# Transposing the probabilities of the last 64 queries of two heads together, and the first two query tiles in one bank, in a block-causal attention kernel with a gated feed-forward

## The chip, the cores and the metric

The kernel runs on one core of one Trainium2 chip. The metric is device time in microseconds of one execution, the median of several runs; lower is better. The engines that work side by side are TensorE (PE in the profile; its weight loads are PEld), VectorE (DVE), ScalarE (ACT), GpSimd (POOL), and SyncE (SP), which here issues transfers. TensorE's results go to PSUM, a memory of eight banks, from which DVE and ACT read them ("evict" them) into SBUF, the working memory.

## What is computed

Attention over 8 batches, 8 heads, 576 tokens and 64 features, in which a query of 64-token block i sees the keys of blocks 0 to i; then a feed-forward network on the concatenated heads, with a convolution of three taps along the tokens as a gate:

```python
scores = scale * np.matmul(q, k.transpose(0, 1, 3, 2))
mask = block_i >= block_j                       # blocks of 64 tokens
scores = np.where(mask, scores, -1000000000.0)
attn = np.exp(scores - np.max(scores, axis=-1, keepdims=True))
attn = attn / (np.sum(attn, axis=-1, keepdims=True) + 1e-09)
x = np.matmul(attn, v)                          # heads side by side: 512 features
...
h = np.maximum(x @ w_in, 0.0)                   # 512 -> 1024
conv_out += conv_w[k][None, None, :] * hp[:, k:k + S, :]   # k = 0, 1, 2
gate = 1.0 / (1.0 + np.exp(-conv_out))
return (h * gate @ w_out).astype(np.float32)    # 1024 -> 512
```

All is float32. To keep precision at TensorE's faster float32r rate, the kernel splits a float32 operand into a high part (rounded to float32r) and a low part (the rest), and sums the products high x high, high x low and low x high.

## The kernel before

**Tiling.** Heads are worked in 32 pairs (two heads of a batch), 64 heads in all. The 576 queries of a head are cut into four tiles of 128 and a last one of 64. Query tile i (0 to 3) sees 128 (i + 1) keys; the last 64 queries see all 576. The last 64 queries of both heads of a pair share one tile of 128 partitions, block 4: rows 0 to 63 belong to the first head and rows 64 to 127 to the second. Their scores and their softmax are made once for the pair, in the first head's turn.

**Stages.** `stage_t` loads q and k of a pair, transposes them (line 476), and splits them (lines 480 and 483) into tiles that transfers copy to where they are needed. `stage_s` makes a head's scores (lines 581, 583; for block 4 line 619), masks (586), takes row maxima (589, 622), exponentials with row sums (592, 633), the reciprocal of the sums (555, 560) and the normalised probabilities `p0` to `p4` (566, on POOL). `stage_x` transposes the probabilities on PE (line 660), so that keys lie along the partitions, and evicts each tile twice: ACT copies the high part out of PSUM (682) and DVE subtracts it from what stands in PSUM to give the low part (685). Tiles 0 and 1 go to `ptah` and `ptal`, tiles 2, 3 and block 4 to `ptbh` and `ptbl`, as [partition, four chunks of 128 keys, 320 queries]. The fifth chunk of keys (64 keys, block 4 alone) stands in an unused corner, chunk 3, columns 0 to 63: its high part on partitions 0 to 63, its low part on 64 to 127. `stage_pv` multiplies by v (725, 732) and evicts into `xt` (743, 746). For the first eight heads, tiles 2 and 3 have their low part made by PE and ACT instead (689, 693), and some banks come from another group.

`ffn` runs for half a batch at a time once the batch's eight heads are done: the first matmul (line 780) for eight groups of 128 features, each with its activation and gate (795 to 821, on ACT, DVE and POOL), and the second matmul (840) with its eviction (850). It runs beside the next batch's attention.

**What sets the order.** No loop is run as written: every step is recorded with an engine, an estimated duration (`c_mm`, `c_act`, `c_dve`, `c_pool`), what it depends on, and a due time. `Plan.order` then simulates the engines with these durations and writes the instructions out, on each engine in the order in which the simulation started them. The feed-forward matmuls are "paced": they fill PE between the others. So an estimated duration that changes can move any instruction. Each engine works its queue in order.

**Buffers.** PSUM's eight banks are given out in three groups: two to `s` (scores), three to `f` (feed-forward), three to `w`, which the transposes of q and k, of the probabilities (`pt`) and the products with v (`tv`) share in turn. `ptah`, `ptal`, `ptbh` and `ptbl` have one buffer each, for all heads in turn.

Of the kernel before, what the change touches and what calls it, by code (L numbers as in the profile page):

```python
# [10 lines left out]
F32R = mybir.dt.float32r  # L11
# [136 lines left out]
def kernel(  # L148
# [85 lines left out]
    def c_dve(n, fast=False):  # L234
        return 0.065 + n / (1920.0 if fast else 960.0)
# [206 lines left out]
    def stage_t(nat, at, first=False):  # L442
# [22 lines left out]
        for which, (n, ld) in enumerate(nat):  # L465
# [4 lines left out]
            for j in range(2):  # L470
# [16 lines left out]
                o = pl.op(ACT, c_act(HS), ev_hi, t0 + 0.5 * j + 0.3, deps=[o], bufs=[tb, hi])  # L487
                es.append(o)
                es.append(pl.op(DVE, c_dve(HS), ev_lo, t0 + 0.5 * j + 0.7, deps=[o], bufs=[tb, hi, lo]))
# [51 lines left out]
    def stage_s(ops, hh, at, early, shared):  # L541
# [8 lines left out]
        def finish(blocks, st, c0, t0):  # L550
# [11 lines left out]
            o = pl.op(DVE, 0.08, i1, t0, deps=exps[4] if blocks[0] == 4 else [exps[x] for x in blocks], bufs=[st])  # L562
            o = pl.op(DVE, 0.09, i2, t0, deps=[o], bufs=[st])
# [8 lines left out]
        for i in range(4):  # L572
# [25 lines left out]
            exps.append(pl.op(ACT, c_act(nk, True, True, True), ex, t0 + 0.6, deps=[o], bufs=[sb, st, pt]))  # L598
# [32 lines left out]
        for j in range(2):  # L631
            def ex4(j=j, sb=banks[j]):
                nc.scalar.activation(out=p4.ap[:, HS * j:HS * j + HS], in_=sb.ap[:, 0:HS], func=AF.Exp,  # L633
                                     bias=st4.ap[:, 2:3], accum_out=st4.ap[:, 4 + j:5 + j])

            es.append(pl.op(ACT, c_act(HS, True, True, True), ex4, t0 + 0.6, deps=[o], bufs=[banks[j], st4, p4]))
# [9 lines left out]
    def stage_x(pbd, hh, at, early):  # L646
        pb, done = pbd
        ta = [one([P, 384], F32R, nm) for nm in ("ptah", "ptal")]
        tb_ = [one([P, 4, 320], F32R, nm) for nm in ("ptbh", "ptbl")]
        evs = []  # L650
        for i in range(5):
            t0 = at + 1.1 * i
            tb = bank("f" if early and i in EFPT else "pt")
            nq = 128 if i < 4 else 64

            def tr(i=i, tb=tb, nq=nq):
                r = slice(64 * hh, 64 * hh + 64) if i == 4 else slice(0, P)
                for c in range(i + 1):
                    kk = 128 if c < 4 else 64
                    nc.tensor.matmul(tb.ap[0:kk, c * nq:(c + 1) * nq], pb[i].ap[r, 128 * c:128 * c + kk],  # L660
                                     ident[r, r], start=(c == 0), stop=True, is_transpose=True,
                                     skip_group_check=True)

            o = pl.op(PE, (i + 1) * (0.109 if i < 4 else 0.056), tr, t0, deps=[done[i]], bufs=[tb, pb[i]])
            nc4 = min(i + 1, 4)

            pth, ptl = ta if i < 2 else tb_

            def chunks(x, i=i, nq=nq, nc4=nc4):
                if i < 2:  # L670
                    return x.ap[:, 128 * i:256 * i + 128].rearrange("p (c n) -> p c n", c=nc4)
                return x.ap[:, 0:nc4, 128 * i - 256:128 * i - 256 + nq]

            parts = [(P, 0, nc4, lambda chunks=chunks, x=pth: chunks(x), lambda chunks=chunks, x=ptl: chunks(x), ptl)]
            if i == 4:
                parts.append((64, 4 * nq, 1, lambda x=pth: x.ap[0:64, 3:4, 0:64], lambda x=pth: x.ap[64:P, 3:4, 0:64], pth))
            for kk, col, nn, hi, lo, lo_t in parts:
                def src(tb=tb, kk=kk, col=col, nn=nn, nq=nq):
                    return tb.ap[0:kk, col:col + nn * nq].rearrange("p (c n) -> p c n", c=nn)

                def ev_hi(src=src, hi=hi):
                    nc.scalar.activation(out=hi(), in_=src(), func=AF.Copy)  # L682

                def ev_lo(src=src, hi=hi, lo=lo):
                    nc.vector.tensor_tensor(out=lo(), in0=src(), in1=hi(), op=ALU.subtract)  # L685

# [271 lines left out]
```

## Time and profile before

| | |
|---|---|
| median of 3 runs | 878.92 us (873.92 to 879.34) |
| profiled execution: its time, its span, mean granted TensorE clock | 879.45 us, 877.7 us, 0.972 |
| half transposes of block 4 (line 660), 64 rows by 128 and 64 keys | 256 + 64 in the trace |
| transposes of 128 x 128 into `w` banks (line 660) | 608 in the trace |
| evictions on ACT (line 682) and on DVE (line 685) in the program | 384 and 368 |

A row of the view by shapes reads: line, engine, operation, output <- input, shapes, count | busy microseconds, mean nanoseconds of one | idle time of the engine before them and what ended it. A row of the view by windows reads: the stretch, its length, then for each engine its busy microseconds and number of instructions, the granted clock, and the transfers' share and GB/s. The chain of waits follows the last instruction back to what released it; a row gives the start, the length and the work. Some matmul records can be missing from a trace, so counts there may fall short of the program's.

### The profile page before, as it was taken

What the parts mean: (1) busy time and instruction counts of PE and PEld (TensorE: products, weight loads), DVE (VectorE), ACT (ScalarE), POOL (GpSimd) and SP (SyncE); (2) the same over time, 40 slices, a digit from 0 to 9 for tenths busy, and PEclk for the clock granted to TensorE, in tenths of its full rate; (3) what the DMA queues carried; (4) which work ended last, traced back from release to release, by engine and by line L of the source; (5) the groups of instructions that cost most, each with busy time, mean ns of one, the idle gap of its engine ahead of it and who ended that gap; (6) DMA issues with size and microseconds to landing.
All of it is one profiled execution on the core that took longest, in us unless ns stands there. A gap on an engine that the chain in (4) does not pass through costs nothing.

```text
span 877.7 us, 17654 instructions
## 1 busy us (share of the span) xinstructions
PE 833.4 (95%) x5393; PEld 726.3 (83%) x5393; DVE 682.9 (78%) x2044; ACT 633.6 (72%) x1894; POOL 463.2 (53%) x615
## 2 busy tenths in 40 slices
PE   4988887899999999999999999999999999999998
PEld 3766776788888979888898979888888979898996
DVE  6677899989796967879796867878796867878541
ACT  5676666678696867878696867878696857878552
POOL 2466786766455434656465434556455534556331
PEclk9987787999999999999999999999999999999999
DMA  8565461554444355454445255454445255540001
GB/s 202 148 159 136 111 182 49 136 134 99 116 102 104 78 135 124 111 131 102 112 94 127 66 136 124 111 133 105 108 101 127 61 136 124 122 99 2 25 24 37
DMA packets 162865, 95.11 MB, mean 108 GB/s; under 512 B 132156, under 2 KB 136276, under 8 KB 162772
## 3 DMA queue, kind: packets, MB, share of 16 engines
q1 hardware_dynamic: 161588, 93.69, 43.9%
q8 instruction: 44, 0.72, 0.4%
q10 hardware_dynamic: 1184, 0.30, 0.2%
q14 instruction: 49, 0.40, 0.1%
HBM read 37.77 MB, written 9.44 MB: 54 GB/s over the span
## 4 chain that ended last, share of the span: by engine, by line
PE 65%; DVE 20%; ACT 10%; issue 3%; DMA 1%; POOL 1%; ACTq 0%; SPq 0%; DVEq 0%; POOLq 0%
PE f L840 19%; PE f L780 11%; PE w L725 8%; PE w L660 8%; PE s L581 4%; PE s L583 3%; PE w L840 3%; DVE st L589 3%; DVE t L802 2%; PE w L476 2%; DVE t L806 2%; DVE ptbl L685 2%; PE s L619 2%; ACT p L592 2%; ACT p L633 2%
## 5 line engine op out<-in xcount | busy, mean ns | idle before, releaser
L566 POOL TENSOR_SCALAR p<-p,st 128x128 f32<-128x128 f32 (+4 forms) x288 | 163.0, 579 | 198.2 <-DVE st L560 125.5
L592 ACT ACTIVATE p<-s,st 128x128 f32<-128x128 f32 (+3 forms) x256 | 134.9, 527 | 55.0 <-DVE st L589 52.3
L821 POOL TENSOR_TENSOR gl<-t,gh 128x288 fp32r<-128x288 f32 x128 | 103.4, 810 | 129.8 <-ACT gh L818 117.7
L660 PE MATMUL w<-ident,p 128*128 128x128 f32 (+1 forms) x928 | 141.3, 266 | 8.2 <-DVE ql L483 2.9
L660 PEld LDWEIGHTS w<-ident,p 128*128 128x128 f32 (+1 forms) x928 | 98.3, 141 | 41.2 <-issue 14.4
L589 DVE TENSOR_REDUCE st<-s 128x1 f32<-128x128 f32 (+3 forms) x256 | 123.5, 484 | 4.4
L682 ACT ACTIVATE ptbh<-w 128x384 fp32r<-128x384 f32 (+3 forms) x248 | 97.0, 419 | 18.2 <-PE w L660 16.9
L840 PE MATMUL f<-woh,gh 128*128 128x512 f32 x248 | 104.4, 421 | 0.0
L685 DVE TENSOR_TENSOR ptbl<-w,ptbh 128x512 fp32r<-128x512 f32 (+1 forms) x176 | 95.2, 541 | 7.7 <-ACT ptbh L682 6.5
L780 PE MATMUL f<-xh,wih 128*128 128x290 f32 x480 | 100.3, 314 | 0.8 <-POOL xh L254 0.3
L780 PE MATMUL f<-xh,wil 128*128 128x290 f32 x480 | 100.1, 313 | 0.0
L840 PE MATMUL f<-wol,gh 128*128 128x512 f32 x248 | 98.6, 398 | 0.0
L840 PE MATMUL f<-woh,gl 128*128 128x512 f32 x248 | 98.6, 398 | 0.0
L780 PE MATMUL f<-xl,wih 128*128 128x290 f32 x480 | 97.3, 309 | 0.0
L583 PE MATMUL s<-kl,qz 128*128 128x128 f32 (+3 forms) x256 | 86.5, 338 | 0.0
L743 ACT ACTIVATE xt<-w 64x256 f32<-64x256 f32 (+1 forms) x128 | 51.3, 401 | 42.8 <-PE w L725 37.6
L780 PEld LDWEIGHTS f<-xh,wih 128*128 128x128 f32 x480 | 74.8, 192 | 5.4 <-DVE t L814 2.2
L802 DVE SCALAR_TENSOR_TENSOR t<-f,cw,t 128x287 f32<-128x287 f32 (+1 forms) x120 | 61.1, 509 | 18.8 <-ACT t L798 17.7
L780 PEld LDWEIGHTS f<-xh,wil 128*128 128x128 f32 x480 | 74.3, 193 | 1.5
L780 PEld LDWEIGHTS f<-xl,wih 128*128 128x128 f32 x480 | 73.8, 192 | 1.1
L746 DVE TENSOR_TENSOR xt<-w,xt 64x256 f32<-64x256 f32 x112 | 51.6, 461 | 26.4 <-ACT xt L743 23.4
L811 ACT ACTIVATE t<-t 128x288 f32<-128x288 f32 x128 | 56.4, 440 | 13.7 <-DVE t L806 13.5
(158 smaller groups left out, 2033.4 us busy)
## 6 DMA issues: line engine op xcount, KB each, us to landing
qn<-in_q_dram SPq DMA_DIRECT2D x64, 144.0 KB, 3.1
out_dram<-stage SPq DMA_DIRECT2D x36, 256.0 KB, 2.3
kn<-in_k_dram SPq DMA_DIRECT2D x62, 144.0 KB, 3.0
ka<-kh SPq DMA_DIRECT2D x62, 144.0 KB, 2.7
kb<-kh SPq DMA_DIRECT2D x62, 144.0 KB, 2.6
vn<-in_v_dram SPq DMA_DIRECT2D x64, 128.0 KB, 2.7
qa<-qh SPq DMA_DIRECT2D x31, 144.0 KB, 3.1
qa<-ql SPq DMA_DIRECT2D x31, 144.0 KB, 3.0
```

The costliest lines, as they stand in the source:

```text
L566: nc.gpsimd.tensor_scalar(out=pt.ap, in0=pt.ap, scalar1=st.ap[:, col:col + 1], scalar2=0.0, op0=ALU.mult, op1=ALU.add)
L583: nc.tensor.matmul(sb.ap[:, 0:nk], qz.ap[:, z:z + 128], kl.ap[:, 0:nk], start=False, stop=True)
L589: nc.vector.tensor_reduce(out=st.ap[:, i:i + 1], in_=sb.ap[:, 0:nk], op=ALU.max, axis=AX.X, negate=True)
L592: nc.scalar.activation(out=pt.ap[:, 0:nk], in_=sb.ap[:, 0:nk], func=AF.Exp, bias=st.ap[:, i:i + 1], accum_out=st.ap[:, 4 + 2 * i:5 + 2 * i])
L660: nc.tensor.matmul(tb.ap[0:kk, c * nq:(c + 1) * nq], pb[i].ap[r, 128 * c:128 * c + kk], ident[r, r], start=(c == 0), stop=True, is_transpo ...
L682: nc.scalar.activation(out=hi(), in_=src(), func=AF.Copy)
L685: nc.vector.tensor_tensor(out=lo(), in0=src(), in1=hi(), op=ALU.subtract)
L725: nc.tensor.matmul(tb.ap[0:m, q0 - qa:qb - qa], vv.ap[:, c, hh, w[part]], pm.ap[:, 128 * c + q0:128 * c + qb] if qa == 0 else pm.ap[:, c, ...
L780: nc.tensor.matmul(fb.ap[:, 0:n2], wt[:, c, fs], xs[c][xi].ap[:, x0:x0 + n2], start=(n + c - c0 == 0), stop=(n + c - c0 == 3 * NCC - 1))
L802: nc.vector.scalar_tensor_tensor(out=t.ap[:, i0:], in0=fb.ap[:, own + i0 - 1:own + HS - 1], scalar=cw[:, f:f + 1], in1=t.ap[:, i0:], op0=A ...
L821: nc.gpsimd.tensor_tensor(out=gbuf[1].ap[:, f, carry:carry + HS], in0=t.ap, in1=gbuf[0].ap[:, f, carry:carry + HS], op=ALU.subtract)
L840: nc.tensor.matmul(fb.ap[:, 0:DM], gbuf[a].ap[:, f, cs], w[:, f, :], start=(f == 0 and n == 0), stop=(f == NFC - 1 and n == 2))
```

## The change

Three things change.

1. *Block 4 once per pair.* In the first head's turn `stage_x` now transposes block 4 with all its 128 rows: four transposes of 128 rows by 128 keys and one of 128 rows by 64 keys, where each head had four of 64 rows by 128 keys and one of 64 by 64. One eviction pair moves 512 columns out of PSUM into both heads' tiles, another the 128 columns of the fifth chunk. The second head's turn transposes tiles 0 to 3 only.
2. *Tiles 0 and 1 together.* The one transpose of tile 0 and the two of tile 1 go into one bank and leave it with one eviction pair of 384 columns instead of 128 and 256.
3. *Buffers and costs.* `ptbh` and `ptbl` become one tile each with a half for each head, so that two heads no longer take turns on one buffer. And the planner's estimates rise: 0.05 us for DVE work with two tensor inputs, 0.02 to 0.08 for several ACT steps, and more for the sums and reciprocals.

Per pair there are 25 transposes where there were 30, and eight eviction pairs where there were twelve; the number of elements moved is the same. The lines move: 660 becomes 672, 725 and 732 become 749 and 756, 743 and 746 become 767 and 770, 780 becomes 804, 795 to 821 become 819 to 845, 840 becomes 864, 850 becomes 874; 682 and 685 stay.

```diff
-    def c_dve(n, fast=False):
-        return 0.065 + n / (1920.0 if fast else 960.0)
+    def c_dve(n, fast=False, two_in=False):
+        return 0.065 + n / (1920.0 if fast else 960.0) + (0.05 if two_in else 0.0)
...
-            o = pl.op(DVE, 0.08, i1, t0, deps=exps[4] if blocks[0] == 4 else [exps[x] for x in blocks], bufs=[st])
-            o = pl.op(DVE, 0.09, i2, t0, deps=[o], bufs=[st])
+            o = pl.op(DVE, 0.15, i1, t0, deps=exps[4] if blocks[0] == 4 else [exps[x] for x in blocks], bufs=[st])
+            o = pl.op(DVE, 0.12, i2, t0, deps=[o], bufs=[st])
...
-    def stage_x(pbd, hh, at, early):
+    ptb_t = [cp.tile([P, 2, 4, 320], F32R, tag=nm, name=nm) for nm in ("ptbh", "ptbl")]
...
+    def stage_x(pbd, hh, at, early, shared):
...
-        tb_ = [one([P, 4, 320], F32R, nm) for nm in ("ptbh", "ptbl")]
+        tb0 = late(0) if hh == 0 else shared[0]
+        tb1 = late(1) if hh == 0 else None
...
-        for i in range(5):
-            t0 = at + 1.1 * i
-            tb = bank("f" if early and i in EFPT else "pt")
-            nq = 128 if i < 4 else 64
...
-                r = slice(64 * hh, 64 * hh + 64) if i == 4 else slice(0, P)
...
+        ea = one_bank([(0, 0, P, 0), (1, 0, P, 128), (1, 1, P, 256)], P, 384, lambda: ta[0].ap, lambda: ta[1].ap,
+                      [done[0], done[1]], at, [pb[0], pb[1]], [ta[0]], [ta[1]], False, "f" if early and 0 in EFPT else "pt", None)
...
+        if hh == 0:
...
+            e4 = one_bank([(4, c, P, 128 * c) for c in range(4)], P, 512,
+                          lambda: tiles[0][:, :, :, 256:320].rearrange("p h c n -> p c h n"),
+                          lambda: tiles[1][:, :, :, 256:320].rearrange("p h c n -> p c h n"), [done[4]], at + 4.2,
+                          [pb[4]], [tb0[0], tb1[0]], [tb0[1], tb1[1]], False, "pt", ("p (c h n) -> p c h n", {"h": 2, "n": 64}))
+            e5 = one_bank([(4, 4, 64, 0)], 64, P, lambda: tiles[0][0:64, :, 3, 0:64], lambda: tiles[0][64:P, :, 3, 0:64],
+                          [done[4]], at + 4.6, [pb[4]], [tb0[0], tb1[0]], [tb0[0], tb1[0]], False, "pt",
+                          ("p (h n) -> p h n", {"h": 2}))
+            shared = (tb1, [e4, e5])
+        return ta, mine, [ea], eb + shared[1], shared
```

The new helper `one_bank` takes a bank, puts a list of transposes into it, and evicts it with one ACT copy and one DVE subtraction (or PE and ACT for the first heads):

```python
def one_bank(trs, rows, n, hi, lo, deps, t0, bufs_p, bufs_hi, bufs_lo, sub_ok, tag, shape):
    tb = bank(tag)
    def tr():
        for z, (x, c, kk, col) in enumerate(trs):
            nc.tensor.matmul(tb.ap[0:kk, col:col + P], pb[x].ap[:, 128 * c:128 * c + kk], ident,
                             start=(z == 0), stop=True, is_transpose=True, skip_group_check=True)
    o = pl.op(PE, len(trs) * 0.109, tr, t0, deps=deps, bufs=[tb] + bufs_p)
...
    e1 = pl.op(ACT, c_act(n) + 0.02, ev_hi, t0 + 0.3, deps=[o], bufs=[tb] + bufs_hi)
...
        e2 = pl.op(DVE, c_dve(n, two_in=True), ev_lo, t0 + 0.5, deps=[e1], bufs=[tb] + bufs_hi + bufs_lo)
```

How the order of the instructions moves is seen at three places. Names in the rows: `w`, `s` and `f` are PSUM banks, `p_...` a probability tile, `ident` the identity matrix, `st_...` the row statistics. A stretch is named by the head (counted from 0) whose scores it begins with; it transposes the head before it.

First, PE in the stretch of head 36, where the second head of a pair is transposed between matmuls of the second feed-forward product. Before:

```order
L660 MATMUL w<-ident,p_6767 128x128 x4
L581 MATMUL s<-ka,qa 128x384
L583 MATMUL s<-kl,qz_88 128x384
L840 MATMUL f<-woh,gh 128x512
L840 MATMUL f<-wol,gh 128x512
L840 MATMUL f<-woh,gl 128x512
L660 MATMUL w<-ident,p_6599 128x64 x4
L660 MATMUL w<-ident,p_6599 64x64
L581 MATMUL s<-ka,qa 128x512
```

And after:

```order
L672 MATMUL w<-ident,p_6451 128x128 x4
L581 MATMUL s<-ka,qa 128x256
L583 MATMUL s<-kl,qz_90 128x256
L864 MATMUL f<-woh,gh 128x512
L864 MATMUL f<-wol,gh 128x512
L864 MATMUL f<-woh,gl 128x512
L581 MATMUL s<-ka,qa 128x384
L583 MATMUL s<-kl,qz_90 128x384
L864 MATMUL f<-woh,gh 128x512
```

The half transposes are gone from this stretch, and the last tile's four transposes stand one score tile earlier.

Second, DVE in the stretch of head 34, beside the activations of the first feed-forward product. Before:

```order
L685 TENSOR_TENSOR ptal<-w,ptah 128x256
L586 MEMSET s 64x64
L589 TENSOR_REDUCE st_100<-s 128x1
L685 TENSOR_TENSOR ptbl<-w,ptbh 128x3x128
L814 SCALAR_TENSOR_TENSOR t<-t,f 128x288
L586 MEMSET s 64x64
L589 TENSOR_REDUCE st_100<-s 128x1
L685 TENSOR_TENSOR ptbl<-w,ptbh 128x4x128
L802 SCALAR_TENSOR_TENSOR t<-f,cw,t 128x287
L685 TENSOR_TENSOR ptbl<-w,ptbh 128x4x64
L806 SCALAR_TENSOR_TENSOR t<-f,cw,t 128x288
L685 TENSOR_TENSOR ptbh<-w,ptbh 64x64
```

And after:

```order
L586 MEMSET s 64x64
L826 SCALAR_TENSOR_TENSOR t<-f,cw,t 128x287
L838 SCALAR_TENSOR_TENSOR t<-t,f 128x288
L589 TENSOR_REDUCE st_102<-s 128x1
L685 TENSOR_TENSOR ptbl<-w,ptbh 128x4x128
L830 SCALAR_TENSOR_TENSOR t<-f,cw,t 128x288
L586 MEMSET s 64x64
L589 TENSOR_REDUCE st_102<-s 128x1
L586 MEMSET s 64x64
L826 SCALAR_TENSOR_TENSOR t<-f,cw,t 128x287
L838 SCALAR_TENSOR_TENSOR t<-t,f 128x288
```

Of five subtractions among the row maxima one is left in these rows; the merged one for tiles 0 and 1 and that for tile 2 stand ahead of them.

Third, PE in the stretch of head 37, where the first head of the pair is transposed beside the first feed-forward product. Before:

```order
L581 MATMUL s<-kb,qb 128x384
L583 MATMUL s<-kl,qz_88 128x384
L780 MATMUL f<-xl,wih 128x290 x2
L660 MATMUL w<-ident,p_6920 128x64 x4
L660 MATMUL w<-ident,p_6920 64x64
L780 MATMUL f<-xh,wih 128x290 x4
```

And after:

```order
L672 MATMUL w<-ident,p_6580 128x128 x4
L581 MATMUL s<-kb,qb 128x384
L583 MATMUL s<-kl,qz_90 128x384
L804 MATMUL f<-xl,wih 128x290 x2
L672 MATMUL w<-ident,p_6580 64x128
L804 MATMUL f<-xh,wih 128x290 x4
```

Block 4 is now transposed here for both heads, in two banks, ahead of and behind the 384-key scores.

More of the change, by code (lines that the diff above doesn't have):

```diff
@@ L640, in stage_s, with late @@
         return pb, done
-    def stage_x(pbd, hh, at, early):
+    ptb_t = [cp.tile([P, 2, 4, 320], F32R, tag=nm, name=nm) for nm in ("ptbh", "ptbl")]
+    def late(hh):
+        res = []
+        for j, nm in enumerate(("ptbh", "ptbl")):
+            x = one([P, 4, 320], F32R, f"{nm}{hh}")
+            x.t = ptb_t[j][:, hh]
+            res.append(x)
+        return res
+    def stage_x(pbd, hh, at, early, shared):
         pb, done = pbd
         ta = [one([P, 384], F32R, nm) for nm in ("ptah", "ptal")]
-        tb_ = [one([P, 4, 320], F32R, nm) for nm in ("ptbh", "ptbl")]
+        tb0 = late(0) if hh == 0 else shared[0]
+        tb1 = late(1) if hh == 0 else None
+        mine = tb0
+        tiles = ptb_t
@@ L702, in stage_x, with tr, src, ev_hi @@
-        return ta, tb_, evs
+        def one_bank(trs, rows, n, hi, lo, deps, t0, bufs_p, bufs_hi, bufs_lo, sub_ok, tag, shape):
+            tb = bank(tag)
+            def tr():
+                for z, (x, c, kk, col) in enumerate(trs):
+                    nc.tensor.matmul(tb.ap[0:kk, col:col + P], pb[x].ap[:, 128 * c:128 * c + kk], ident,
+                                     start=(z == 0), stop=True, is_transpose=True, skip_group_check=True)
+            o = pl.op(PE, len(trs) * 0.109, tr, t0, deps=deps, bufs=[tb] + bufs_p)
+            def src():
+                x = tb.ap[0:rows, 0:n]
+                return x.rearrange(shape[0], **shape[1]) if shape else x
+            def ev_hi():
+                nc.scalar.activation(out=hi(), in_=src(), func=AF.Copy)
+            def ev_lo():
+                nc.vector.tensor_tensor(out=lo(), in0=src(), in1=hi(), op=ALU.subtract)
+            def sub():
+                for c in range(n // P):
+                    nc.tensor.matmul(tb.ap[:, 128 * c:128 * c + P], nident, hi()[:, c], start=False, stop=True,
+                                     skip_group_check=True)
+            def ev_lo2():
+                nc.scalar.activation(out=lo(), in_=src(), func=AF.Copy)
+            e1 = pl.op(ACT, c_act(n) + 0.02, ev_hi, t0 + 0.3, deps=[o], bufs=[tb] + bufs_hi)
+            if sub_ok:
+                e2 = pl.op(PE, n // P * c_mm(P, 0), sub, t0 + 0.4, deps=[e1], bufs=[tb] + bufs_hi)
+                e2 = pl.op(ACT, c_act(n), ev_lo2, t0 + 0.5, deps=[e2], bufs=[tb] + bufs_lo)
+            else:
+                e2 = pl.op(DVE, c_dve(n, two_in=True), ev_lo, t0 + 0.5, deps=[e1], bufs=[tb] + bufs_hi + bufs_lo)
+            return e1, e2
@@ new lines, in stage_x, with view @@
+        by_c = ("p (c n) -> p c n", {"n": P})
+        ea = one_bank([(0, 0, P, 0), (1, 0, P, 128), (1, 1, P, 256)], P, 384, lambda: ta[0].ap, lambda: ta[1].ap,
+                      [done[0], done[1]], at, [pb[0], pb[1]], [ta[0]], [ta[1]], False, "f" if early and 0 in EFPT else "pt", None)
+        eb = []
+        for i in (2, 3):
+            def view(x, i=i):
+                return x.ap[:, 0:i + 1, 128 * i - 256:128 * i - 128]
+            eb.append(one_bank([(i, c, P, 128 * c) for c in range(i + 1)], P, 128 * (i + 1),
+                               lambda view=view: view(mine[0]), lambda view=view: view(mine[1]), [done[i]],
+                               at + 1.4 * (i - 1), [pb[i]], [mine[0]], [mine[1]], early and i in EBLK,
+                               "f" if early and i in EFPT else "pt", by_c))
@@ L716, in stage_pv @@
             cs = [c for c in range(4) if 128 * c < qb]
-            need = [evs[i] for i in range(len(evs)) if qa < 128 * i + 128 and 128 * min(i, 4) < qb]
+            need = x[2] if qa == 0 else x[3]
             o = None
```

62 lines of the change are left out of this document (14 added, 48 removed).

## Prediction

> **What bounds the kernel now.** I read the page first, for busy shares and the chain that ended last, then the stages by windows, then the chain inside single stages, and last the groups by shape. From the page:
>
> ```profile
> span 877.7 us, 17654 instructions
> PE 833.4 (95%) x5393; PEld 726.3 (83%) x5393; DVE 682.9 (78%) x2044; ACT 633.6 (72%) x1894; POOL 463.2 (53%) x615
> ...
> PEclk9987787999999999999999999999999999999999
> ...
> PE 65%; DVE 20%; ACT 10%; issue 3%; DMA 1%; POOL 1%; ACTq 0%; SPq 0%; DVEq 0%; POOLq 0%
> ```
>
> TensorE (PE) carries 65% of the chain, VectorE and ScalarE together 30%. That is an average over stages with different limits. The view by windows cuts one batch at the start of each head's first score matmul (five of its eight heads below; columns: stretch, length, then PE, PE loads, DVE, ACT, POOL busy); the last two rows are the first and the last of the six equal batches that follow the first 216 us:
>
> ```profile
> 441.45:453.59 12.14, 12.14 (x96) 11.65 (x95) 11.76 (x37) 11.07 (x36) 5.84 (x9) 1.00 0.17 43
> 453.59:465.38 11.79, 11.56 (x74) 9.56 (x72) 9.80 (x32) 9.52 (x31) 8.75 (x12) 1.00 0.79 178
> 465.38:478.06 12.68, 12.68 (x82) 10.52 (x81) 8.84 (x29) 7.81 (x24) 4.29 (x8) 1.00 0.23 60
> 478.06:490.25 12.19, 12.16 (x93) 11.57 (x92) 10.18 (x30) 9.86 (x31) 8.22 (x11) 1.00 0.85 207
> 490.25:505.24 14.99, 14.73 (x106) 13.16 (x105) 13.41 (x41) 13.28 (x42) 7.37 (x11) 1.00 0.02 4
> ...
> 216.00:314.80 98.80, 97.52 (x661) 86.01 (x660) 81.35 (x246) 75.61 (x231) 53.82 (x74) 1.00 0.45 106
> ...
> 708.40:806.80 98.40, 97.83 (x657) 86.74 (x656) 78.14 (x242) 73.92 (x224) 49.41 (x69) 1.00 0.39 94
> ```
>
> PE's busy time counts matmuls that overlap, so it tells little; DVE's does. In 465.38 to 478.06, where the second feed-forward matmul (L840) fills PE, DVE works 8.84 of 12.68 us. In 441.45 to 453.59 and 490.25 to 505.24, where the first one (L780) runs and brings its activation work along, DVE works 97% and 89%, ACT 91% and 89%. The chain says the same. In the L840 stretch it is PE alone; here its line shares and the four places that the change touches:
>
> ```profile
> by line: PE f L840 52.1%; PE w L725 11.9%; PE w L660 11.3%; PE w L476 8.8%; PE s L619 6.5%; PE s L581 6.2%; PE s L583 5.0%; PE w L732 0.3%
> ...
> 465.40 0.22 PE w L660 x2
> ...
> 466.55 0.33 PE w L660 x3
> ...
> 467.81 0.44 PE w L660 x4
> ...
> 469.29 0.45 PE w L660 x5
> ```
>
> In the L780 stretch it soon leaves PE and goes through DVE, instruction after instruction, with the evictions of the transposed probabilities among them:
>
> ```profile
> 444.65 0.19 PE s L583
> ...
> 445.61 0.27 DVE ptbl L685
> ...
> 446.63 0.33 DVE ptbl L685
> 446.96 0.42 DVE t L806
> ...
> 447.42 0.22 DVE ptbh L685
> ```
>
> By the chain view of each, heads 32, 33, 35, 36 and 39 of this batch (stretches from 418.02, 430.71, 453.59, 465.38 and 505.24) are paced mainly by PE, heads 34, 37 and 38 (from 441.45, 478.06, 490.25) by DVE and ACT.
>
> **The change part by part.** A stretch transposes the probabilities of the head before it, so odd stretches serve the first head of a pair and even ones the second. Durations by shape, DVE then ACT:
>
> ```profile
> L685 DVE TENSOR_TENSOR ptbl<-w,ptbh 128x512 fp32r<-128x512 f32 x56 | 38.2, 682 | 3.6 <-ACT ptbh L682 3.0
> L685 DVE TENSOR_TENSOR ptbl<-w,ptbh 128x384 fp32r<-128x384 f32 x56 | 30.7, 548 | 1.8 <-ACT ptbh L682 1.7
> L685 DVE TENSOR_TENSOR ptbl<-w,ptbh 128x256 fp32r<-128x256 f32 x64 | 26.4, 413 | 2.2 <-ACT ptbh L682 1.8
> L685 DVE TENSOR_TENSOR ptal<-w,ptah 128x256 fp32r<-128x256 f32 x64 | 26.4, 413 | 1.3 <-ACT ptah L682 1.3
> L685 DVE TENSOR_TENSOR ptal<-w,ptah 128x128 fp32r<-128x128 f32 x56 | 16.0, 285 | 1.3 <-ACT ptah L682 0.7
> L685 DVE TENSOR_TENSOR ptbh<-w,ptbh 64x64 fp32r<-64x64 f32 x64 | 14.0, 218 | 1.3
> ...
> L682 ACT ACTIVATE ptbh<-w 128x512 fp32r<-128x512 f32 x64 | 38.3, 598 | 3.8 <-PE w L660 2.9
> L682 ACT ACTIVATE ptbh<-w 128x384 fp32r<-128x384 f32 x56 | 27.8, 496 | 6.4 <-PE w L660 6.2
> L682 ACT ACTIVATE ptbh<-w 128x256 fp32r<-128x256 f32 x64 | 24.6, 384 | 8.1 <-PE w L660 7.8
> L682 ACT ACTIVATE ptah<-w 128x256 fp32r<-128x256 f32 x64 | 24.5, 383 | 11.2 <-PE w L660 11.1
> L682 ACT ACTIVATE ptah<-w 128x128 fp32r<-128x128 f32 x56 | 15.2, 271 | 2.1 <-PE w L660 2.1
> L682 ACT ACTIVATE ptbh<-w 64x64 fp32r<-64x64 f32 x64 | 13.4, 209 | 0.0
> ```
>
> *Evictions.* Before, each head pays on DVE 285+413+548+682+413+218 = 2559 ns and on ACT 271+383+496+598+384+209 = 2341 ns. After, the second head pays 548+548+682 = 1778 on DVE and 496+496+598 = 1590 on ACT: 0.78 and 0.75 us less. The first head pays 548+548+682, then 682 for the shared block and one 64x128 piece that no row shows: at least the 64x64 row (218), at most the 128x128 row (285), and 285 is nearest, since time goes with the columns. That is 2745, 0.19 us more on DVE; on ACT 1590+598+271 = 2459, 0.12 more. The shared block is written in runs of 64 elements over two halves. A price for that would show between block 4 before (runs of 64: 413 and 384) and blocks of the same 256 elements in runs of 128 (413 and 383): none.
>
> *Transposes.* In the chain four 128x128 ones take 0.44 us, three 0.33, two 0.22: 0.11 each. Five half ones take 0.45: 0.09 each. So a head costs 10 x 0.11 + 0.45 = 1.55 us before. After, the second head costs 10 x 0.11 = 1.10, that is 0.45 less, and the first 14 x 0.11 plus one with 64 columns of weights. That one takes 0.09 to 0.11 by the same rows; at 0.11 the first head comes to 1.65, 0.10 more. The Trainium skill speaks against this gain: its page "TensorE: Matmul & The Clock Gate", section "Back-to-back issue gap", gives 60 cycles for up to 64 moving columns and 134 for 128, by which five full ones would cost slightly more than ten half ones and the sum below would end at 871. The 0.09 against 0.11 here disagrees, and the same page's section "LDWEIGHTS" tells why, since a load's time goes with its columns, which the half ones did not halve.
>
> *Moved work, waits, queues.* The second head's block 4 is transposed and evicted a stretch earlier, with the first's; its normalisation on POOL already preceded the first's transposes. No DMA and no POOL instruction is added or dropped, and their queues keep their sequence there. New waits: the transposes of block 0 now wait for block 1's normalisation as well, which POOL does behind it:
>
> ```profile
> L566 POOL TENSOR_SCALAR p<-p,st 128x256 f32<-128x256 f32 x64 | 31.4, 491 | 0.0
> ```
>
> These 0.49 us of latency are covered by the L840 or L780 matmuls that stand between, and without them would be 0.49 us of PE for each head. And the shared eviction needs the previous pair's second product to have read its half, which stands in the stretch before. Behind a late eviction on ACT wait the exponentials, and behind those the next score matmul. The probability tiles no longer alternate on one buffer, which costs nothing and frees no wait that the trace shows.
>
> *The planner's costs.* They rise for DVE with two inputs, ACT and the sums, so that every engine's order is recomputed. Feed-forward matmuls per stretch stay about as they were where I compared (equal counts at every head border of this batch). I take nothing for this: better timed orders and unlucky ones are both possible. Its bounds are below.
>
> *The sum.* Per batch: heads 34 and 38 save 0.78 each on DVE (1.56), head 37 loses 0.19; on PE heads 32 and 36 save 0.45 each (0.90), heads 33, 35 and 39 lose 0.10 each (0.30). Together 1.97, say 2.0 us, over six batches 12.0. The first 216 us hold 16 heads, eight pairs: nothing at the least, since they wait much for transfers and weights, and at most 0.6 a pair, 4.8; I take 2.5. The last 71 us hold nearly no attention: 0. The profiled run took 879.45 us (its span 877.7 and 1.75 around it), 0.5 above the median of 878.92. 879.45 - 14.5 = 865.
>
> **The rivals.** *DVE's gain meets the next limit.* When DVE and ACT get lighter in heads 34, 37 and 38, PE is close behind (12.14 of 12.14 us by its overlapping count). Then those heads gain only PE's 0.45 and lose 0.10, and the first 16 heads nothing: 2 x 0.45 - 0.10 + 0.60 = 1.4 a batch, 8.4 in all, 871. For it: PE's busy column. Against it: in the chain quoted above DVE's work follows upon DVE's work, with no PE row between. *PE's part gains nothing*, where a half transpose takes half of a full one's 0.11 us and ten of them no more than five full ones: only 1.56 - 0.19 = 1.4 a batch and nothing early, also 871; the 0.45 us for five speak against it. The Trainium skill's table named above is a rule that would bring this. *A better order.* The three heads paced by DVE last 39.32 us, in which DVE works 35.35; the truer costs could close half of the 4 us of gaps: 2.0 a batch, 12 in all, 853.
>
> *Slower: banks held longer.* Transposes, loads of q and k, and products share three PSUM banks; PE stands still when the bank next in turn is not evicted. A merged tile is held for ACT and then DVE: blocks 0 and 1 for 496+548 ns where they had 556 and 796, the shared block for 598+682 where it had 797. That is 0.25 us longer for each head, 0.48 for each pair, 0.98 a pair in all, 31 us over 32 pairs if PE waits every time: 865 + 31 = 896. With half of them waited for it is 881, and that is about where the sign turns. What PE waited for between 180 and 806.8 us speaks against it:
>
> ```profile
> PEld w L476 <- DVE xt L746: 6.4, 17, 0.5
> ...
> PE w L660 <- DVE ql L483: 1.8, 3, 0.6
> ...
> PEld w L660 <- DVE ptbl L685: 0.2, 1, 0.2
> ```
>
> Evictions of transposes held PE up once, for 0.2 us, and a pair now takes 16 turns of the banks where it took 18. But 16 is no multiple of three, so the banks that meet now shift from pair to pair.
>
> **How the numbers follow.** My forecast has 0.54, the next limit 0.16, PE gaining nothing 0.04, the better order 0.15, the banks 0.11. A measurement of this kernel tells about 1% from no change, 8.8 us. Forecast, better order and a part of the 871 cases (which stand at the border) are faster by over 1%: 0.72. The rest of these and the banks below half are within: 0.20. Banks waited for nearly always, 0.08, are slower. The likeliest time is 865, its own range 860 to 870; the range that holds 8 in 10 reaches from the better order to the banks waited for in a third of the cases, 853 to 876.
>
> **What would show it.** Rows by shape: L682 of 256 instructions and L685 of 240 where 384 and 368 stood, with the shared 128x512 and the first 128x384 at the old durations. Windows: even stretches shorter by some 0.5 to 0.8 us, odd ones the same within 0.2, and a batch of 96.4 instead of 98.4. Chain: PE's share up, DVE's and ACT's down. Waits: no more than a few us of PE for L685. Wrong it would be if PE waits on L685 by tens of us, if the 512-wide shared eviction takes over 0.75 us, or if the batches stay at 98 us with fewer busy microseconds, which would mean that the gain went into gaps.

## The result, and the profile after

The changed kernel takes 835.39 us (median of 4 runs, 835.12 to 836.09) where the kernel before takes 876.42 beside it: a ratio of 0.9533 with a 95% interval of 0.9491 to 0.9574. It is 41 us faster, where 14.5 were forecast and 853 was the lower end of the range. The profiled execution took 836.09 us, its span is 834.3. Among the runs described further on, two executions (one of e12_after_costs_twice and one of the kernel before beside it) took 2874 and 2624 us and are in no median here.

The page of the changed kernel, the rows that answer to those of before:

```profile
span 834.3 us, 16929 instructions
...
PE 791.4 (95%) x5233; PEld 717.0 (86%) x5233; DVE 656.7 (79%) x1916; ACT 623.9 (75%) x1766; POOL 461.9 (55%) x615
...
PE 87%; ACT 5%; DVE 4%; POOL 1%; DMA 1%; issue 1%; SPq 0%; ACTq 0%; DVEq 0%; POOLq 0%
```

DVE works 26 us less and ACT 10 us less. The chain is another one too: PE carries 87% of it instead of 65%, and DVE and ACT together 9% instead of 30%. The same stretches of one batch in the view by windows (length, then PE, PE loads, DVE, ACT, POOL busy):

```profile
419.50:430.50 11.00, 11.00 (x86) 10.88 (x85) 10.65 (x32) 10.53 (x33) 5.79 (x9) 1.00 0.17 44
430.50:442.10 11.60, 11.60 (x80) 10.32 (x78) 10.37 (x33) 9.94 (x29) 8.82 (x12) 1.00 0.77 180
442.10:453.95 11.85, 11.85 (x76) 10.17 (x74) 8.03 (x25) 7.35 (x21) 4.70 (x8) 1.00 0.25 63
453.95:465.90 11.95, 11.95 (x94) 11.78 (x93) 10.28 (x29) 10.19 (x30) 7.75 (x11) 1.00 0.82 198
465.90:478.92 13.02, 13.02 (x96) 12.40 (x95) 11.87 (x38) 12.01 (x37) 6.62 (x10) 1.00 0.08 18
```

These are the stretches of heads 34 to 38. Head 34 went from 12.14 to 11.00 us, head 38 from 14.99 to 13.02, and DVE is now at 97% and 91% there without setting the pace: the chain of head 34's stretch holds PE rows alone. Its line shares:

```profile
by line: PE f L804 56.5%; PE w L749 13.7%; PE s L619 7.3%; PE w L672 7.0%; PE s L581 5.9%; PE s L583 5.8%; PE w L476 4.5%; PE w L756 0.3%
```

Head 36, where PE set the pace before and after, went from 12.68 to 11.85, 0.83 less where I had 0.45. That is the first sign of a wrong price. The evictions have the durations that I took, by shape (L682 is ACT, L685 DVE):

```profile
L685 DVE TENSOR_TENSOR ptbl<-w,ptbh 128x512 fp32r<-128x512 f32 x88 | 59.7, 679 | 1.7 <-ACT ptbh L682 1.4
L682 ACT ACTIVATE ptbh<-w 128x512 fp32r<-128x512 f32 x96 | 57.5, 600 | 14.1 <-PE w L672 13.5
L685 DVE TENSOR_TENSOR ptal<-w,ptah 128x384 fp32r<-128x384 f32 x56 | 31.1, 555 | 4.4 <-ACT ptah L682 3.5
...
L682 ACT ACTIVATE ptah<-w 128x384 fp32r<-128x384 f32 x56 | 27.4, 490 | 5.5 <-PE w L672 5.5
...
L685 DVE TENSOR_TENSOR ptbh<-w,ptbh 64x128 fp32r<-64x128 f32 x32 | 9.1, 284 | 1.0
...
L682 ACT ACTIVATE ptbh<-w 64x128 fp32r<-64x128 f32 x32 | 8.6, 268 | 4.6 <-PE w L672 4.5
```

The shared block, written in runs of 64 over two halves, costs no more than a plain one (679 against 682, 600 against 598; the rows of 88 and 96 hold 32 shared blocks beside the plain ones), and the 64x128 piece costs what its columns say (284 and 268 against the 285 and 271 that I took).

### The profile page after: what moved, and what is told of

It reads as the page before. It is cut to its first block, busy times and chain, and to the rows that moved or that the text cites. A ratio compares the mean times of both kernels' runs of the same rounds, so it can differ in the third digit from the quotient of the medians.

```text
span 834.3 us, 16929 instructions
## 1 busy us (share of the span) xinstructions
PE 791.4 (95%) x5233; PEld 717.0 (86%) x5233; DVE 656.7 (79%) x1916; ACT 623.9 (75%) x1766; POOL 461.9 (55%) x615
## 4 chain that ended last, share of the span: by engine, by line
PE 87%; ACT 5%; DVE 4%; POOL 1%; DMA 1%; issue 1%; SPq 0%; ACTq 0%; DVEq 0%; POOLq 0%
PE f L804 23%; PE f L864 21%; PE w L749 12%; PE w L672 9%; PE s L581 5%; PE s L583 5%; PE w L476 3%; PE w L864 3%; PE s L619 3%; PE s L804 2%; ACT p L592 1%; ACT ptbh L682 1%; DMA qn<-in_q_dram 1%; DVE stage L326 0%; ACT ptbl L693 0%
## 5 line engine op out<-in xcount | busy, mean ns | idle before, releaser
L566 POOL TENSOR_SCALAR p<-p,st 128x256 f32<-128x256 f32 (+4 forms) x288 | 162.2, 577 | 177.1 <-DVE st L560 139.5
L672 PE MATMUL w<-ident,p 128*128 128x128 f32 (+1 forms) x752 | 121.1, 276 | 4.6 <-DVE ptbl L685 1.6
L682 ACT ACTIVATE ptbh<-w 128x512 fp32r<-128x512 f32 (+1 forms) x184 | 92.0, 508 | 25.0 <-PE w L672 24.3
L672 PEld LDWEIGHTS w<-ident,p 128*128 128x128 f32 (+1 forms) x752 | 91.2, 141 | 15.4 <-DVE ptbl L685 1.8
L804 PE MATMUL f<-xh,wih 128*128 128x290 f32 x480 | 96.2, 311 | 1.1 <-DVE t L838 1.1
L804 PE MATMUL f<-xl,wih 128*128 128x290 f32 x480 | 94.9, 307 | 0.0
L804 PE MATMUL f<-xh,wil 128*128 128x290 f32 x480 | 93.5, 306 | 0.0
L685 DVE TENSOR_TENSOR ptbl<-w,ptbh 128x512 fp32r<-128x512 f32 (+1 forms) x144 | 89.0, 627 | 2.8 <-ACT ptbh L682 2.3
L767 ACT ACTIVATE xt<-w 64x256 f32<-64x256 f32 (+1 forms) x128 | 51.3, 401 | 35.0 <-PE w L749 31.8
```

What stands on the lines that cost most here:

```text
L566: nc.gpsimd.tensor_scalar(out=pt.ap, in0=pt.ap, scalar1=st.ap[:, col:col + 1], scalar2=0.0, op0=ALU.mult, op1=ALU.add)
L672: nc.tensor.matmul(tb.ap[0:kk, col:col + P], pb[x].ap[:, 128 * c:128 * c + kk], ident, start=(z == 0), stop=True, is_transpose=True, skip_ ...
L804: nc.tensor.matmul(fb.ap[:, 0:n2], wt[:, c, fs], xs[c][xi].ap[:, x0:x0 + n2], start=(n + c - c0 == 0), stop=(n + c - c0 == 3 * NCC - 1))
```

## The experiments

Two questions were open: how much came from the new planner costs, which I had priced at nothing, and how much from the fewer transposes and evictions; and what of the latter. Four groups ran, e1 to e4, e5 to e8, e9 to e12 and e13 to e15, each beside its own runs of the kernel before (medians 878.63, 874.25, 878.67 and 878.19 us), against which the gains stand. Between runs of different groups the ratios are the better measure, so that both are given below where it matters.

| run | median us | gain us | ratio to before, 95% interval |
|---|---|---|---|
| e1_costs_only | 857.60 | 21.0 | 0.9762 (0.9731 to 0.9793) |
| e2_structure_only | 854.42 | 24.2 | 0.9719 (0.9678 to 0.9760) |
| e3_block4_only | 841.93 | 36.7 | 0.9575 (0.9549 to 0.9601) |
| e4_merge01_only | 858.27 | 20.4 | 0.9748 (0.9695 to 0.9802) |
| e5_rows128_per_head | 848.97 | 25.3 | 0.9676 (0.9625 to 0.9726) |
| e6_extra_half | 853.78 | 20.5 | 0.9736 (0.9696 to 0.9776) |
| e7_extra_full | 840.37 | 33.9 | 0.9578 (0.9538 to 0.9617) |
| e8_extra_narrow | 840.01 | 34.2 | 0.9570 (0.9527 to 0.9613) |
| e9_costs_ffn | 872.15 | 6.5 | 0.9926 (0.9897 to 0.9956) |
| e10_costs_attention | 859.58 | 19.1 | 0.9791 (0.9728 to 0.9855) |
| e11_costs_twice | 875.00 | 3.7 | 0.9957 (0.9925 to 0.9989) |
| e12_after_costs_twice | 843.95 | 34.7 | 0.9617 (0.9572 to 0.9661) |
| e13_costs_pv | 872.38 | 5.8 | 0.9943 (0.9917 to 0.9970) |
| e14_costs_softmax_split | 866.80 | 11.4 | 0.9879 (0.9823 to 0.9935) |
| e15_after_no_ffn_costs | 840.05 | 38.1 | 0.9585 (0.9537 to 0.9633) |

### The costs alone, the structure alone

The costs alone, on the kernel before:

```diff
-            o = pl.op(DVE, 0.08, i1, t0, ...)
+            o = pl.op(DVE, 0.15, i1, t0, ...)
-            o = pl.op(ACT, c_act(n), ev0, at + 0.6, deps=[o], bufs=[tb, xt])
+            o = pl.op(ACT, c_act(n) + 0.08, ev0, at + 0.6, deps=[o], bufs=[tb, xt])
...
```

> The kernel before with the raised planner costs alone (the same numbers, on the same steps); transposes, evictions and buffers as before. Theory A (the order made from truer costs closes the gaps that DVE and ACT leave in the stretches of the first feed-forward product): most of the 41 us comes here, 845 to 852 us, and the chain of those stretches turns to PE. Theory B (fewer and larger evictions take DVE and ACT below PE in those stretches, the costs do little): 870 to 880 us, chain as before. Theory C (each alone gives a part): 855 to 868.

The structure alone is the changed kernel with these lines turned back:

```diff
-        return 0.065 + n / (1920.0 if fast else 960.0) + (0.05 if two_in else 0.0)
+        return 0.065 + n / (1920.0 if fast else 960.0)
...
```

> The changed kernel with the planner costs of before; transposes, evictions, buffers and due times as changed. Theory A: only the work that my sum counted, 860 to 868 us. Theory B: nearly all of the gain, 835 to 842 us, PE's share of the chain near 87%. Theory C: 845 to 858.

They took 857.60 and 854.42 us: each alone gives a bit more than half of the whole, 21 and 24 us, and together they give 41, about 4 less than their sum. Theory C held; neither A nor B. In these two runs it is the costs that take DVE and ACT off the chain. First the costs alone, then the structure alone (chain by engine):

```profile
PE 86%; DVE 5%; ACT 5%; DMA 1%; issue 1%; POOL 1%; SPq 1%; ACTq 0%; DVEq 0%; POOLq 0%
```

```profile
PE 64%; DVE 17%; ACT 13%; issue 3%; DMA 1%; POOL 1%; SPq 1%; ACTq 0%; DVEq 0%; POOLq 0%
```

The structure alone has 21 us less DVE work than before (662.1 against 682.9 busy) and still a chain with 30% of DVE and ACT; the costs alone have the same 2044 DVE instructions as before (670.3 us busy) and 10%. The lengths of the eight stretches, in us, from the starts of each head's first score matmul:

| head | before | costs alone | structure alone | changed | my change | structure minus before |
|---|---|---|---|---|---|---|
| 32 | 12.69 | 12.49 | 12.04 | 11.86 | -0.45 | -0.65 |
| 33 | 10.74 | 10.61 | 10.83 | 10.77 | +0.10 | +0.09 |
| 34 | 12.14 | 12.16 | 11.87 | 11.00 | -0.78 | -0.27 |
| 35 | 11.79 | 11.17 | 11.43 | 11.60 | +0.10 | -0.36 |
| 36 | 12.68 | 12.46 | 12.05 | 11.85 | -0.45 | -0.63 |
| 37 | 12.19 | 11.91 | 12.28 | 11.95 | +0.19 | +0.09 |
| 38 | 14.99 | 14.06 | 14.09 | 13.02 | -0.78 | -0.90 |
| 39 | 12.90 | 12.28 | 12.56 | 12.53 | +0.10 | -0.34 |

Heads 32 and 36, purely PE's, shorten by 0.65 and 0.63 where I had counted 0.45: 0.2 us of PE are missing in my price of a group of half transposes.

### Block 4 joint, tiles 0 and 1 joint

Block 4 joint, with tiles 0 and 1 apart:

```diff
-        ea = one_bank([(0, 0, P, 0), (1, 0, P, 128), (1, 1, P, 256)], P, 384, ...)
+        ea0 = one_bank([(0, 0, P, 0)], P, 128, ...)
+        ea = one_bank([(1, 0, P, 0), (1, 1, P, 128)], P, 256, ...)
```

> The changed kernel with tiles 0 and 1 apart again (two banks, two eviction pairs per head: 0.15 us of DVE and 0.16 us of ACT more per head), block 4 joint, new costs and buffers. Theory A: close to the changed kernel, 838 to 846 us, since the order matters more than the work. Theory B: DVE and ACT work comes back at 64 x 0.15 = 10 us, 845 to 858 us.

Tiles 0 and 1 joint, with block 4 for each head:

```diff
-            e4 = one_bank([(4, c, P, 128 * c) for c in range(4)], P, 512, ...)
+                nc.tensor.matmul(tb.ap[0:kk, 64 * c:64 * c + 64], pb[4].ap[r, 128 * c:128 * c + kk], ident[r, r], ...)
+        e4 = evict(P, 0, 4, lambda: mine[0].ap[:, :, 256:320], lambda: mine[1].ap[:, :, 256:320], mine[0], mine[1])
```

> The changed kernel with block 4 transposed and evicted for each head apart again (in one bank with two eviction pairs, as before), tiles 0 and 1 joint, new costs and a half of ptbh and ptbl for each head. It brings back 0.35 us of PE and about 0.3 us of DVE and of ACT per pair, 11 and 10 us in all. Theory A: 845 to 852 us. Theory B: 845 to 858 us, and together with the run on block 4 the two parts add up to what the structure gives.

841.93 and 858.27 us, the first where theory A has it, the second just above what either expected. Joining tiles 0 and 1 without block 4, with the half buffers and the costs, is no better than the costs alone (858.27 against 857.60). Joining block 4 with tiles 0 and 1 apart takes 15.7 us off the costs alone (857.60 to 841.93), in the same group; with tiles 0 and 1 joint it takes off 19 by the ratios (0.9748 to 0.9533) and 22.9 by the medians. On PE, which carries the chain in all of these, I had priced block 4 at 0.35 us a pair, 11 us in all. So 5 to 12 us of what it gives had no price on PE in my sum.

### What a half transpose costs

The chain of the kernel before shows it one row behind the row that I quoted for the five half transposes (469.29, 0.45 us), where I had not looked:

```profile
469.74 0.43 PE s L581
470.17 0.23 PE s L583
```

The matmul behind the group takes 0.43 us, its twin with the same shape 0.23. With the costs alone the same shows where other work follows: a group, then three feed-forward matmuls that take 0.90 us, and three of the same a little later that take 0.69:

```profile
446.75 0.45 PE w L660 x5
447.20 0.90 PE f L840 x3
448.10 0.23 PE s L581
448.33 0.23 PE s L583
448.56 0.69 PE f L840 x3
```

So a group costs 0.45 + 0.20 = 0.65 us, within 0.02 us of what heads 32 and 36 shortened by. Four runs test what brings the 0.20. The first transposes block 4 for each head with all its rows:

```diff
+        f4 = one_bank([(4, c, P, 128 * c) for c in range(4)], P, 256, ...,
+                      lambda tb: tb.ap.rearrange("p (c n) -> p c n", n=P)[:, :, own])
+        f5 = one_bank([(4, 4, 64, 0)], 64, 64, ..., lambda tb: tb.ap[0:64, own])
```

> The changed kernel with block 4 for each head apart, like the run that merges tiles 0 and 1 only, but each head's turn transposes all 128 rows (four of 128 by 128 and one of 128 by 64 keys) and evicts its own 64 columns. Beside that run it has five transposes of 128 rows per head in place of five of 64 rows, and one more turn of a bank. Theory S (a transpose costs PE its spacing in the chain, 0.11 us for 128 rows and 0.09 for 64): 64 x 5 x 0.02 = 6 us slower than that run, about 864 us. Theory R (going from 64 rows of the array back to 128 costs PE another 0.2 us, seen in the chain as a matmul that takes 0.42 instead of 0.23 behind the half transposes): 64 x 0.2 = 13 us less and 6 more, about 851 us.

The others add one transpose per head to the changed kernel, ahead of tile 2's, with the order of all else as it was; of 64 rows, of 128 rows, and of 128 rows by 64 keys:

```diff
+                    nc.tensor.matmul(tb.ap[:, 0:64], pb[2].ap[0:64, 0:P], ident[0:64, 0:64], ...)   # half
+                    nc.tensor.matmul(tb.ap[:, 0:P], pb[2].ap[:, 0:P], ident, ...)                   # full
+                    nc.tensor.matmul(tb.ap[0:64, 0:P], pb[2].ap[:, 0:64], ident, ...)               # narrow
```

> The changed kernel, its order untouched, with one more transpose of 64 rows by 128 keys at the head of tile 2's transposes (its result is overwritten by them), 64 in all. Theory S: 64 x 0.09 = 6 us over the changed kernel, about 841 us. Theory R: 64 x 0.29 = 18.5 us, about 854 us, as far as PE is the bound.

> The same with one more transpose of 128 rows by 128 keys at that place. Theories S and R alike: 64 x 0.11 = 7 us, about 842 us. It is the control for the half one: under R it is 11 us faster than that, under S 1 us slower.

> The same with one more transpose of 128 rows by 64 keys (64 columns of weights) at that place. Theory S and theory R in rows: 4 to 7 us, 839 to 842 us. If narrow weights bring the 0.2 us as well as few rows do: about 854 us.

Theory R held in all four. 320 larger transposes in place of 320 half ones made the kernel faster: 848.97 us beside 858.27, where R expected 851 and S 864; by the ratios (0.9676 and 0.9748) it is 6 us, with intervals that overlap a little. 64 half transposes cost 18.4 us over the changed kernel by the medians and 17.8 by the ratios, 0.28 to 0.29 each; 64 full ones 5.0 and 3.9, 0.06 to 0.08 each; 64 narrow ones 4.6 and 3.2. The traces give these prices more sharply, without the first 216 us: from the first score matmul of head 16 to that of head 63, with 47 added transposes between, the changed kernel takes 547.0 us, that with the half ones 562.6, with the full ones 552.1, with the narrow ones 551.9. That is 0.33, 0.11 and 0.10 us for each. The half and the full ones ran in one group, 13.4 us apart, with intervals (0.9696 to 0.9776 and 0.9538 to 0.9617) that lie apart. The chain of the run with the half one, at tile 2 of head 32, then those with the full and with the narrow one at the same place, and the changed kernel without any:

```profile
415.85 0.20 PE w L672
416.05 0.47 PE w L675 x3
```

```profile
411.28 0.12 PE w L672
411.40 0.33 PE w L675 x3
```

```profile
411.16 0.11 PE w L672
411.27 0.33 PE w L675 x3
```

```profile
410.15 0.34 PE w L672 x3
```

Line 672 is the added one in the first three. The half one takes 0.20 us itself and makes the three behind it 0.14 longer; the full one takes 0.12, the narrow one 0.11, and both leave the three as they were. So it is not the number of weight columns: the narrow one loads 64 of them and has no such price. What the half one has alone is 64 rows, and with them 64 columns of the identity that move past the weights, where the other two have 128 of both. No run parts the rows from these moving columns; I go on speaking of rows.

### Which costs, and how far

On the kernel before, the raised costs of the feed-forward activations alone, of attention alone, and all of them with each raise doubled; and the doubled raises on the changed kernel:

```diff
-            o = pl.op(DVE, c_dve(HS), c2, clock + 1, deps=[o], bufs=[fb, t])
+            o = pl.op(DVE, c_dve(HS, two_in=True) + 0.02, c2, clock + 1, deps=[o], bufs=[fb, t])      # e9
...
-            o = pl.op(DVE, 0.08, i1, t0, ...)
+            o = pl.op(DVE, 0.15, i1, t0, ...)                                                         # e10
...
+            o = pl.op(DVE, 0.22, i1, t0, ...)                                                         # e11, e12
```

> The kernel before with the raised costs of the feed-forward activations alone (relu, the two taps, the gate product). The raised costs together gave 21 us. Theory F (DVE's load in the first product's stretches was underrated by the feed-forward steps, so exponentials were put into ACT's queue ahead of row maxima that DVE had not reached): 858 to 863 us and ACT's wait of the exponentials for the row maxima down as in that run. Theory P (no step is special, any change of the order gives some part): 865 to 875.

> The kernel before with the raised costs of the attention steps alone (splitting q, k and probabilities, sums, exponentials, product evictions). Theory F: 868 to 878 us. Theory P: 865 to 875, the two parts adding up to about 21 us or not at all. If attention's costs are the ones that were wrong: 858 to 863.

> The kernel before with every raise doubled. Theory T (the raise helps because the costs come nearer to the measured durations): overshoot gives part of it back, 860 to 870 us. Theory H (any higher estimate for DVE and ACT helps, since it holds back work that then waits in a queue): 850 to 858 us. Theory L (luck of an order): anywhere from 855 to 885.

> The changed kernel with every raise doubled. Theory T: 838 to 845 us. Theory H: 828 to 835 us, faster than the changed kernel. Theory L: 835 to 860 us. Where PE is the bound in nearly all stretches already, as the changed kernel's chain says (PE 87%), little can be gained: 832 to 840.

Attention's costs give 19.1 us, the feed-forward's 6.5, both 21.0: theory F fell, and attention's are the estimates that mattered most. Doubling the raises leaves 3.7 of the 21, and on the changed kernel it costs 7.4 us by the ratios (0.9617 and 0.9533) and 8.6 by the medians. So theory H fell: a higher estimate does not help as such. Theory T has the sign of both and the size of the second; the first, 875.00, lies beyond its 870. Both lie within what mere luck of an order (L) allows. How near the estimates came to the measured durations, the rows of the kernel before say. The sums stood at 80 ns, now at 150, doubled at 220; the reciprocals at 90, now 120; the eviction of 320 columns of the product on DVE at 398, now 518, doubled 638:

```profile
L555 DVE TENSOR_REDUCE st<-st 128x1 f32<-128x2 f32 (+2 forms) x160 | 24.3, 152 | 36.3 <-ACT p L592 17.4 <-ACT p L633 16.3 <-POOL p L566 0.2
L560 DVE RECIPROCAL st<-st 128x1 f32<-128x1 f32 (+1 forms) x160 | 26.0, 162 | 2.9
...
L746 DVE TENSOR_TENSOR xt<-w,xt 64x320 f32<-64x320 f32 x56 | 27.7, 494 | 13.3 <-ACT xt L743 11.8
L802 DVE SCALAR_TENSOR_TENSOR t<-f,cw,t 128x288 f32<-128x288 f32 x60 | 30.7, 511 | 14.1 <-ACT t L798 13.5
L814 DVE SCALAR_TENSOR_TENSOR t<-t,f 128x288 f32<-128x288 f32 x120 | 53.7, 447 | 6.5 <-ACT t L811 4.8
```

Measured are 152 ns for the sums, 162 for the reciprocals and 494 for the eviction: the raise meets the first, is 42 short of the second and 24 above the third, and the doubled raise overshoots the first and the third. Most of the other raised steps lie the other way. A tap of the convolution (line 802) stood at 365, now 435, doubled 505, and takes 511; the gate's product (line 814) stood at 365, now 415, doubled 465, and takes 447; the eviction of 256 transposed columns on DVE stood at 332, now 382, doubled 432, and takes 413. By these means the doubled estimates are the nearer ones there, as they are for the other evictions of transposes, and yet doubling lost most of the gain. So nearness to the profile's means, which is theory T, does not explain these runs. Nor is the mean the only measure: in the chain quoted ahead of the result a tap holds DVE for 0.42 us. Which duration a planner should be given stays open. The last runs part the attention costs, and take the feed-forward costs off the changed kernel:

```diff
-            o = pl.op(ACT, c_act(n), ev0, at + 0.6, deps=[o], bufs=[tb, xt])
+            o = pl.op(ACT, c_act(n) + 0.08, ev0, at + 0.6, deps=[o], bufs=[tb, xt])                   # e13
...
-            exps.append(pl.op(ACT, c_act(nk, True, True, True), ex, t0 + 0.6, ...))
+            exps.append(pl.op(ACT, c_act(nk, True, True, True) + 0.03, ex, t0 + 0.6, ...))            # e14
...
-            o = pl.op(ACT, c_act(n2) + 0.04, relu, clock, deps=[o, wdone["cw"]], bufs=[fb])
+            o = pl.op(ACT, c_act(n2), relu, clock, deps=[o, wdone["cw"]], bufs=[fb])                  # e15
```

> The kernel before with the raised costs of the two evictions of the product with v alone (0.08 us on ACT, 0.12 on DVE). The attention costs together gave 18 us. Theory V (these two are the raises that lie farthest from the old estimates, and the planner put the next score steps too early behind them): 858 to 864 us. Theory D (the raise counts wherever an estimate was short, each part gives a part): 866 to 873 us.

> The kernel before with the other raised attention costs alone (splitting q, k and the probabilities, sums and reciprocals, exponentials). Theory V: 872 to 878 us. Theory D: 864 to 872 us, and its gain and that of the run on the product's evictions add up to about 18 us. If they do not add up, what counts is the order that results and not any one estimate.

> The changed kernel without the raised costs of the feed-forward activations. On the kernel before these gave 6 us alone and 2 us on top of the attention costs. If they add up: 836 to 842 us. If only the order that results counts: anywhere from 830 to 850, perhaps faster than the changed kernel.

5.8 and 11.4 us: together 17.2 of the 19.1 of attention, and with the 6.5 of the feed-forward 23.7 where all together give 21.0. Theory D held and V fell: each part gives its part. That three parts nearly add up speaks against L, though it does not exclude that luck has a share in each: in the traces between heads 16 and 63 they gain 3.7, 8.8 and 7.5 us, in sum 20.0 where all together gain 15.5. On the changed kernel the feed-forward costs are worth some 5 us (840.05 against 835.39), as either expectation allows, and the two intervals overlap.

One reading of mine did not hold. I had thought that ACT's queue was the place: exponentials that stand ahead of other work and wait for row maxima which DVE has not reached. From 180 to 740 us that wait fell from 42.0 us before to 25.9 with the costs alone:

```profile
ACT p L592 <- DVE st L589: 42.0, 77, 1.1
```

```profile
ACT p L592 <- DVE st L589: 25.9, 47, 1.1
```

But with the doubled costs it is the shortest of all, and that kernel is hardly faster than before:

```profile
ACT p L592 <- DVE st L589: 13.8, 25, 1.4
```

So this wait goes along with the gain in one case and not in the other. The shares of the chain do no better. The kernel before with the doubled costs, 3.7 us faster, and then the changed kernel without the feed-forward's costs, 38.1 us faster:

```profile
PE 84%; DVE 6%; ACT 2%; POOL 2%; issue 2%; DMA 2%; SPq 0%; ACTq 0%; DVEq 0%; POOLq 0%
```

```profile
PE 64%; DVE 16%; ACT 14%; issue 2%; POOL 2%; DMA 1%; SPq 0%; ACTq 0%; DVEq 0%; POOLq 0%
```

The slower of the two has DVE and ACT off the chain, the faster one has them on it. That the raised costs are worth 21 us is shown; through which wait they are is not settled.

## Why the prediction was wrong

**The direction and the place of the work** were right: PE in the stretches of the second product, DVE and ACT in three of eight, and a gain on each. So were the prices of all evictions, those that no row had shown included. Head by head the fit is poorer. With the structure alone head 38 gained 0.90 for 0.78, but head 34 only 0.27 for 0.78. Heads 33 and 37 lost 0.09 each where 0.10 and 0.19 were foreseen, but heads 35 and 39 gained 0.36 and 0.34 where a loss of 0.10 was; since the losses of 0.10 rest on the wrong price below, the fit of head 33 is luck. A batch (from head 16 to head 56, five batches) took 98.9 us before and takes 93.4, where 98.4 and 96.4 were forecast.

**"I take nothing for this"** is the step that failed most. The planner's costs gave 21 us alone. The rival that stood for them, the better order, had the sign, and its 12 us were bounded by half of DVE's idle time in three stretches of a batch. That bound was too narrow in kind. Of the 2.98 us that these eight heads gained with the costs alone, heads 34, 37 and 38 have 1.19; heads 35, 36 and 39 gained 0.62, 0.22 and 0.62. The first 16 heads came 6.5 us earlier to their end (head 16 starts at 214.0 instead of 220.5), in part perhaps by a higher granted clock. DVE's idle time in the stretches that DVE paces did not bound what an order can give; why the new order is better stays open.

**"Five half ones take 0.45: 0.09 each"** was read from the chain one row too short. A group costs 0.65 with what it does to the matmul behind it. A pair then costs 20 x 0.11 + 2 x 0.65 = 3.50 us of PE before and 2.75 after: 0.75 less and not the 0.35 that followed from my prices, 12.8 us more over 32 pairs. For heads 32 and 36 it gives the 0.65 and 0.63 within 0.02. For the first head of a pair it turns my loss of 0.10 into a gain of 0.10 (1.75 before, 1.65 after). In the five heads that PE paces it adds 1.0 us to my 1.97 a batch, to 2.97; the structure alone gained 15.3 us from head 16 to head 63, 2.6 for eight heads. The row that could have warned me stood in the same view; and the view by shapes had 11.0 us of idle time, put down to issue, ahead of the half transposes' weight loads, in a row that I did not quote.

**The rule of the Trainium skill** that I weighed, a table of isolated gaps ("TensorE: Matmul & The Clock Gate", section "Back-to-back issue gap"), would have half transposes cost less than half of full ones. The runs say the opposite: 0.28 to 0.33 us for an added half one, 0.06 to 0.11 for an added full one. I had put it down to the weight loads, by the same page's section "LDWEIGHTS". The narrow one, whose load has half the columns, saves next to nothing beside the full one, so that no run here shows the loads to be what sets the price.

**The first 216 us**, which I sized at 2.5 of at most 4.8, gave 10.1 in the changed kernel (head 16 starts at 210.4), 11.8 with the structure alone (208.8). How much of it is work, how much order and how much the granted clock is not separated: from 120 to 180 us the clock was 0.84 before, 0.86 with the costs alone, 0.97 with the structure alone, 0.89 in the changed kernel.

**The rivals.** The next limit did come up behind DVE, PE in all eight stretches; but it stood lower than I thought, since the half transposes, dearer than I had them, were gone from it. The banks were hardly waited for: the largest wait of the transposes for an eviction by DVE is 3.4 us in all, two waits. Joining tiles 0 and 1 gave nothing on top of the costs alone and 4 to 6.5 us on top of block 4 (0.9575 to 0.9533, 841.93 to 835.39), with intervals that overlap.

**The sum of the halves.** By the medians the halves do not add up, 21.0 + 24.2 against 41.0. From the first score matmul of head 16 to that of head 63 they do: 578.8 us before, 563.4 with the costs alone, 563.5 with the structure alone, 547.0 with both, so 15.5 + 15.3 against 31.8. What does not add up is the time to head 16, 6.5 + 11.8 against 10.1, in which the granted clock differed between the profiled executions as told above; from 220 us on it was 1.00 in all four. Single heads do not add up either (head 34: 0.02 longer with the costs alone, 0.27 shorter with the structure alone, 1.14 shorter with both), which fits orders that move work from stretch to stretch.

## What to carry to other kernels

Price an operation by what the chain does from the row ahead of it to the row behind it, not by its own rows: here 0.20 of the 0.65 us that a group of half-height transposes cost stood in the next matmul. Where a planner orders the work by estimated durations, the estimates are a part of the kernel and have to be measured like one: here one set of raises was worth nearly as much as the change of the work itself, raises twice as large lost most of that again, and neither the profile's means nor the chain's shares told which would do. A change that touches both has to be priced as two changes, each measured alone.

## What the runs showed of the hardware

A transpose of 64 rows, with 64 moving columns, set between work that uses 128 rows, costs 0.28 to 0.33 us of the kernel's time (18 us for 64 of them), in the chain 0.20 for itself and 0.14 for those behind it; with 128 of both it costs 0.06 to 0.11. A weight load of 64 columns beside 128 makes next to no difference (4.6 against 5.0 us for 64 of them). That half the rows cost more than all of them I had not expected.
